# Order of the second-layer groups, GELU passes and first-batch steps in a fused attention and MLP kernel

The kernel runs on one core of a Trainium2 chip. The metric is the device time of one execution in microseconds (us): the median of several runs. Profiles and traces are of one run each (for the kernel before a further one, of 464.52 us), and the span of a profile is about 2 us shorter than the time of the same run.

## The reference

Attention whose softmax has an additional 1 in the denominator, then a two-layer MLP with exact GELU on the heads put side by side:

```
q, k, v: (8, 12, 448, 64)       # batch, heads, sequence, head size, fp32
scores = q @ k^T / 8;  m = max(scores)
e = exp(scores - m);   attn = e / (sum(e) + exp(-m) + 1e-9)
x = (attn @ v), heads joined    # 3584 tokens x 768
h = x @ w_in                    # 768 x 2048
out = gelu(h) @ w_out           # 2048 x 768, fp32
```

The kernel works in fp16 with fp32 sums and replaces the row's maximum by a constant shift.

## The kernel before

The eight batches are cut into 48 steps, one for each pair of heads. In step s the engines compute the scores and exps of pair s and the value products of pair s-1; the MLP of the batch before is laid between them as filler for the matmul engine (PE). Scores go to `st` tiles, of which there are two, and everything else of PE goes to four single banks.

```python
def scores(g, half):                       # 2 st tiles, 4 matmuls, 2 exps
    for j in (2 * half, 2 * half + 1):
        st = ps_st.tile([P, 2, 512], FP32, name="st")            # ps_st has bufs=2
        for e in range(2):
            nc.tensor.matmul(st[0:PS, e, 0:S], kt[r, c, j, :], qt[r, c]...)       # L179
        nc.scalar.activation(out=et_t[g][:, j], in_=st[...], func=AF.Exp, ...)    # L183

def attend(g):                             # 8 value products, 2 sums
    ...                                                                           # L208
    nc.tensor.matmul(den[...], ones, sum_t[g][:, e, :], ...)                      # L214
    nc.scalar.activation(out=rec, in_=den[:, 0:S], func=AF.Ln, bias=oneb)         # L218
    nc.scalar.activation(out=rec, in_=rec, func=AF.Exp, scale=-1.0)               # L219
    nc.vector.tensor_tensor(out=xt_t[b][:, c, :], in0=po[:, 0:S], in1=rec, op=ALU.mult)

def step(s, items):
    n = len(items) // 2
    scores(s, 0)
    if s < NPAIR - 1:
        transpose_on_pe(0, s + 1)
    for f in items[:n]:                    # first part of the filler
        f()
    presum(s, 0)                           # DVE adds exps for the sums
    attend(s - 1)
    scores(s, 1)
    if 2 <= s < 2 + NPAIR:
        transpose_on_pe(1, s - 2)
    for f in items[n:]:                    # second part of the filler
        f()
    presum(s, 1)
```

(The conditions for the first and last step are left out.) An item is either a chunk of the first layer (`layer1`: 6 matmuls of 448 columns, L237, there are 16 chunks to a batch) or half a row tile of the second layer (16 matmuls of 384 columns, L282). Exp and Ln share one table of ScalarE (ACT), and GELU needs another one. So GELU is done in one pass for each batch: load the table, apply it to the chunks that wait in a buffer, do the remaining chunks straight from PSUM, load the table back. The second-layer items of the batch become available after its pass.

```python
def gelu_window(b, n):
    load_table(SET_GELU)
    for f in take(len(l2)):                # second-layer items that are left
        f()
    ...                                    # n buffered chunks, then 16 - n direct ones
    load_table(SET_LN_EXP)
    l2.extend(layer2_items(b))
...
    if r < 3:
        step(s, mlp1(b, f0, f1))           # first-layer chunks as filler
    else:
        step(s, take((len(l2) - 2) // (6 - r)))   # second-layer items as filler
    if r in (1, 2) and b + 2 < B:
        transpose_on_dma(b + 2, r - 1)     # queries at r=1, keys at r=2
        if r == 2 and b + 4 < B:
            load_qk(b + 4)
    if r == 2:
        gelu_window(b, f1)                 # NBURST = 12: 12 buffered, 4 direct
```

The queries and keys of batches 0 and 1 are transposed by PE, those of later batches by the DMA queues (`transpose_on_dma`, issued by SyncE). Loads into the raw buffers are issued by GpSimd (POOL) and wait until the transposes of the batch two before have read their buffer.

The softmax here doesn't subtract the row's maximum and nothing guards it: scores larger than these inputs give would overflow.

Of the kernel before, what the change touches and what calls it, by code (L numbers as in the profile page):

```python
# [19 lines left out]
def kernel(  # L20
# [17 lines left out]
    NPAIR = H // 2  # L38
    MCH = DM // P
    FCH = DFF // P  # L40
# [28 lines left out]
    def load_table(set_id):  # L69
        nc.scalar.add_instruction(  # L70
            mybir.InstLoadActFuncSet(
                name=nc.get_next_instruction_name(),
                act_func_set_id=set_id,
                engine=mybir.EngineType.Activation,
                ins=[],
                outs=[],
            )
        )
# [7 lines left out]
    def load_heads(pool, name, tiles, key, src, h0=0, h1=H):  # L86

        if key not in tiles:
            tiles[key] = pool.tile([PS, H, NJ, D], FP16, name=name)
        nc.gpsimd.dma_start(  # L90
            out=tiles[key][:, h0:h1],
            in_=src[key[0]].rearrange("h (p j) d -> p h j d", j=NJ)[:, h0:h1],
        )

    def load_qk(b, *heads):
        for w, src in (("q", q), ("k", k)):
            load_heads(raw_pool, f"raw{w}", raw_t, (b, w), src, *heads)

    def load_v(b, *heads):
        load_heads(v_pool, "vn", v_t, (b,), v, *heads)  # L100
# [43 lines left out]
    def transpose_on_pe(b, c):  # L144
        for w in range(2):
            src = raw_t[b, "qk"[w]]
            tp = ps_bank.tile([P, NJ, PS], FP16, name="bank")
            for j in range(NJ):
                for e in range(2):
                    nc.tensor.transpose(  # L150
                        tp[e * D:(e + 1) * D, j, :], src[:, 2 * c + e, j, :], ident
                    )
            nc.vector.tensor_copy(out=qt_t[b][w][:, c], in_=tp)
# [16 lines left out]
    def scores(g, half):  # L170
        b, c = divmod(g, NPAIR)
        qt, kt = qt_t[b]
        if half == 0:
            et_t[g] = et_pool.tile([PS, NJ, 2, S], FP16, name="et")
        for j in (2 * half, 2 * half + 1):
            st = ps_st.tile([P, 2, 512], FP32, name="st")
            for e in range(2):
                r = slice(e * D, (e + 1) * D)
                nc.tensor.matmul(  # L179
                    st[0:PS, e, 0:S], kt[r, c, j, :],  # L180
                    qt[r, c].rearrange("p j s -> p (j s)"), start=True, stop=True,
                )
            nc.scalar.activation(  # L183
                out=et_t[g][:, j], in_=st[0:PS, :, 0:S], func=AF.Exp,
                bias=expb[0:PS], scale=scale,
            )

    def presum(g, part):

        et = et_t[g]  # L190
        if part == 0:
            sum_t[g] = [sum_pool.tile([PS, 2, 2, S], FP16, name="t2"), None]
        t2 = sum_t[g][0]
        nc.vector.tensor_tensor(  # L194
            out=t2[:, part], in0=et[:, 2 * part], in1=et[:, 2 * part + 1], op=ALU.add)
        if part == 1:
            sum_t[g] = sum_pool.tile([PS, 2, S], FP16, name="ksum")
            nc.vector.tensor_tensor(out=sum_t[g], in0=t2[:, 0], in1=t2[:, 1], op=ALU.add)  # L198

    def attend(g):  # L200
        b, c = divmod(g, NPAIR)
        if c == 0:
            xt_t[b] = xt_pool.tile([P, MCH, S], FP16, name="xt")
        et = et_t.pop(g)
        po = ps_bank.tile([P, 512], FP32, name="bank")
        for j in range(NJ):
            for e in range(2):
                nc.tensor.matmul(  # L208
                    po[e * D:(e + 1) * D, 0:S], v_t[b,][:, 2 * c + e, j, :], et[:, j, e, :],
                    start=(j == 0), stop=(j == NJ - 1),  # L210
                )
        den = ps_bank.tile([P, 512], FP32, name="bank")
        for e in range(2):
            nc.tensor.matmul(  # L214
                den[e * D:(e + 1) * D, 0:S], ones, sum_t[g][:, e, :], start=True, stop=True,
            )
        rec = rec_pool.tile([P, S], FP32, name="rec")
        nc.scalar.activation(out=rec, in_=den[:, 0:S], func=AF.Ln, bias=oneb, scale=1.0)  # L218
        nc.scalar.activation(out=rec, in_=rec, func=AF.Exp, scale=-1.0)  # L219
        nc.vector.tensor_tensor(out=xt_t[b][:, c, :], in0=po[:, 0:S], in1=rec, op=ALU.mult)  # L220
# [1 line left out]

    gt_even = gt_pool.tile([P, FCH, NFULL], FP16, name="gt_even")
    gt_odd = gt_pool.tile([P, FCH, LEFT + S], FP16, name="gt_odd")
    NBURST = 12
    h_t = {}

    def gelu_out(b, f0, f1):

        if b % 2 == 0:  # L230
            return [(0, NFULL, gt_even[:, f0:f1, :]), (NFULL, S, gt_odd[:, f0:f1, 0:LEFT])]
        return [(0, S, gt_odd[:, f0:f1, LEFT:])]

    def layer1(b, fc, direct=False):
        ph = ps_bank.tile([P, 512], FP32, name="bank")
        for m in range(MCH):
            nc.tensor.matmul(  # L237
                ph[:, 0:S], w_in_sb[:, m, fc * P:(fc + 1) * P], xt_t[b][:, m, :],
                start=(m == 0), stop=(m == MCH - 1),
            )  # L240
        if direct:
            for c0, c1, dst in gelu_out(b, fc, fc + 1):
                nc.scalar.activation(out=dst[:, 0, :], in_=ph[:, c0:c1], func=AF.Gelu)  # L243
        else:
            if fc == 0:
                h_t[b] = h_pool.tile([P, NBURST, S], FP32, name="hbuf")
            nc.vector.tensor_copy(out=h_t[b][:, fc, :], in_=ph[:, 0:S])  # L247

    def gelu_burst(b, f0, f1):
        for c0, c1, dst in gelu_out(b, f0, f1):  # L250
            nc.scalar.activation(out=dst, in_=h_t[b][:, f0:f1, c0:c1], func=AF.Gelu)  # L251
# [46 lines left out]
    NSTEP = B * NPAIR  # L298
    l2 = []

    def step(s, items):
        n = len(items) // 2
        if s < NSTEP:
            scores(s, 0)
        if s < NPAIR - 1:
            transpose_on_pe(0, s + 1)
        for f in items[:n]:
            f()
        if s < NSTEP:
            presum(s, 0)  # L310
        if s >= 1:
            attend(s - 1)
        if s < NSTEP:
            scores(s, 1)
        if 2 <= s < 2 + NPAIR:
            transpose_on_pe(1, s - 2)
        for f in items[n:]:
            f()
        if s < NSTEP:
            presum(s, 1)  # L320

    def mlp1(b, f0, f1):
        return [lambda fc=fc: layer1(b, fc) for fc in range(f0, f1)]

    def take(n):
        got = l2[:n]
        del l2[:n]
        return got

    def gelu_window(b, n):  # L330

        load_table(SET_GELU)
        for f in take(len(l2)):
            f()
        if b == 0:
            for i in range(FCH - n):
                gelu_burst(b, i * n // (FCH - n), (i + 1) * n // (FCH - n))
                layer1(b, n + i, direct=True)
        else:
            for f0 in range(0, n, 6):  # L340
                gelu_burst(b, f0, min(f0 + 6, n))
            for fc in range(n, FCH):
                layer1(b, fc, direct=True)
        load_table(SET_LN_EXP)
        l2.extend(layer2_items(b))
# [2 lines left out]
    transpose_on_pe(0, 0)  # L348
    alloc_qt(1)
    for s in range(NPAIR):  # L350
        step(s, [])
    for b in (2, 3):
        load_qk(b)

    for s in range(NPAIR, NSTEP + 1):
        b, r = divmod(s - 1 - NPAIR, NPAIR)
        if b < 0:
            step(s, [])
            for f in mlp1(0, 0, 2):
                f()  # L360
            continue
        f0, f1 = 4 * r, min(4 * r + 4, NBURST)
        if b == 0:
            f0, f1 = min(f0 + 2, 10), min(f1 + 2, 10)
        if r < 3:
            step(s, mlp1(b, f0, f1))
        else:
            n = len(l2) - 2
            step(s, take(n // (6 - r)))
        if r == 0 and b + 2 < B:  # L370
            load_v(b + 2)
        if r in (1, 2) and b + 2 < B:
            transpose_on_dma(b + 2, r - 1)
            if r == 2 and b + 4 < B:
                load_qk(b + 4)
        if r == 2:
            gelu_window(b, f1)

    load_table(SET_GELU)
# [36 lines left out]
```

## Time and profile before

| | before |
|---|---|
| time, three runs | 464.41 us (462.44 to 465.28) |
| span of the profile | 462.8 us |
| PE busy, idle | 431.7 us, 31.1 us |
| mean granted PE clock | 0.988 |

The prediction shows the page's busy shares, its slices and four stretches, and the timeline of PE at two GELU passes. Two lines of the list of waits of the kernel before complete them (waiting engine, tile and line; what it waited for; us in total, times, longest us):

```profile
PE st L179 <- ACT et L183: 15.7, 18, 4.8
...
ACT rec L218 <- PE bank L214: 68.2, 39, 3.9
```

The first is what PE lost to full score tiles: half of its idle time. The second is ACT's wait for the sums. It is longer, but ACT is busy only 68% of the span, so that wait costs something only where PE in its turn waits for the exps behind it.

### The profile page before, as it was taken

The page shows a single profiled execution, that of the slowest core. Times are in us where ns is not written, and L with a number is a line of the kernel's source. Part 1 is how long each engine was busy: PE and PEld are TensorE (multiplying, and loading weights), DVE is VectorE, ACT ScalarE, POOL GpSimd, SP SyncE. Part 2 cuts the span into 40 slices and gives each one's busy share as a digit, 9 for nine tenths or more (in the row PEclk, how much of TensorE's full clock was granted, in tenths as well). Part 3 has the DMA queues.
Part 4 walks back from the last instruction along what each step waited for, and adds up shares of the span by engine and source line. Part 5 has one row for each costly group of instructions (what it writes and reads, how often), then busy time and mean ns, then how long its engine had stood idle before and what let it go on. Part 6 is the DMA issues. An engine that isn't in the chain of part 4 may idle for free.

```text
span 462.8 us, 6665 instructions
## 1 busy us (share of the span) xinstructions
PE 431.7 (93%) x2720; PEld 214.2 (46%) x2720; DVE 211.2 (46%) x381; ACT 314.4 (68%) x398; POOL 32.5 (7%) x43
## 2 busy tenths in 40 slices
PE   3888996899999999799999999799999999799995
PEld 1343443354555445354555445354555445355563
DVE  1464672346714574356724574246814573330021
ACT  3778679676877669876876668776877668844200
POOL 8310020000100000000100000000000000000000
PEclk9999999799999999999999999899999999999999
DMA  8999999942792609941891606033351201020022
GB/s 103 194 206 206 209 198 186 141 69 60 109 164 55 110 3 176 96 82 47 109 164 48 115 14 142 1 61 69 59 95 43 61 2 32 4 66 3 27 77 68
DMA packets 75119, 42.51 MB, mean 92 GB/s; under 512 B 34128, under 2 KB 71504, under 8 KB 75088
## 3 DMA queue, kind: packets, MB, share of 16 engines
q0 software_dynamic: 37968, 22.81, 37.1%
q1 hardware_dynamic: 37120, 19.27, 19.8%
q8 instruction: 21, 0.34, 0.3%
q14 instruction: 10, 0.08, 0.1%
HBM read 45.61 MB, written 11.01 MB: 122 GB/s over the span
## 4 chain that ended last, share of the span: by engine, by line
PE 84%; ACT 7%; DMA 4%; DVE 2%; POOL 2%; issue 1%; POOLq 0%
PE bank L282 33%; PE bank L237 31%; PE st L179 9%; PE bank L208 8%; DMA rawk<-in_k_dram 4%; ACT et L183 3%; PE bank L214 2%; ACT L70 1%; PE bank L150 1%; ACT gt_even L243 1%; DVE ksum L198 1%; ACT gt_even L251 1%; POOL rawq L90 1%; DVE osb L286 1%; DVE t L194 1%
## 5 line engine op out<-in xcount | busy, mean ns | idle before, releaser
L183 ACT ACTIVATE et<-st,expb 112x896 f16<-112x896 f32 x192 | 181.5, 999 | 26.6 <-PE st L179 26.5
L237 PE MATMUL bank<-xt,w_in_sb 128*128 128x448 f16 x768 | 154.1, 353 | 0.6 <-ACT gt_odd L243 0.4
L237 PEld LDWEIGHTS <-w_in_sb 128*128 128x128 f16 x768 | 71.6, 98 | 75.0 <-issue 12.9
L282 PE MATMUL bank<-w_out_sb,gt_odd 128*128 128x384 f16 x512 | 87.0, 327 | 0.0
L286 DVE COPY osb<-bank 128x384 f32<-128x384 f32 x56 | 31.2, 557 | 118.9 <-PE bank L282 118.9
L179 PE MATMUL st<-tq,tk 64*112 64x448 f16 x384 | 66.2, 407 | 16.2 <-ACT et L183 15.7
L194 DVE TENSOR_TENSOR t<-et 112x896 f16<-112x896 f16 x96 | 59.3, 618 | 43.5 <-ACT et L183 43.4
L218 ACT ACTIVATE rec<-bank,oneb 128x448 f32<-128x448 f32 x48 | 30.4, 633 | 68.2 <-PE bank L214 68.2
L282 PE MATMUL bank<-w_out_sb,gt_even 128*128 128x384 f16 x384 | 69.9, 341 | 0.0
L282 PEld LDWEIGHTS <-gt_odd 128*128 128x128 f16 x512 | 48.6, 98 | 37.1 <-issue 6.1
L247 DVE COPY hbuf<-bank 128x448 f32<-128x448 f32 x82 | 50.4, 621 | 17.6 <-PE bank L237 17.1
L220 DVE TENSOR_TENSOR xt<-bank,rec 128x448 f16<-128x448 f32 x48 | 30.0, 625 | 55.7 <-ACT rec L219 55.7
L282 PEld LDWEIGHTS <-gt_even 128*128 128x128 f16 x384 | 37.6, 101 | 29.9 <-issue 8.3
L208 PE MATMUL bank<-et,vn 112*64 112x448 f16 x384 | 50.0, 387 | 0.0
L179 PEld LDWEIGHTS <-tk 64*112 64x112 f16 x384 | 22.5, 133 | 55.6 <-issue 52.1
L243 ACT ACTIVATE gt_odd<-bank 128x448 f16<-128x448 f32 (+1 forms) x46 | 19.4, 421 | 18.4 <-PE bank L237 18.1
L198 DVE TENSOR_TENSOR ksum<-t 112x896 f16<-112x896 f16 x48 | 30.0, 625 | 1.8
L208 PEld LDWEIGHTS <-vn 112*64 112x64 f16 x384 | 19.1, 117 | 23.9 <-issue 16.2
L219 ACT ACTIVATE rec<-rec 128x448 f32<-128x448 f32 x48 | 27.7, 577 | 1.5
L70 ACT ACT_TABLE_LOAD x16 | 20.5, 1283 | 1.0 <-PEq L400 0.7
L214 PE MATMUL bank<-ksum,ones 112*64 112x448 f16 x96 | 18.6, 382 | 2.0 <-DVE ksum L198 2.0
L251 ACT ACTIVATE gt_odd<-hbuf 128x2688 f16<-128x2688 f32 (+3 forms) x18 | 19.3, 1086 | 0.0
(25 smaller groups left out, 110.1 us busy)
## 6 DMA issues: line engine op xcount, KB each, us to landing
rawq<-in_q_dram POOLq DMA_DIRECT2D x7, 672.0 KB, 12.9
rawk<-in_k_dram POOLq DMA_DIRECT2D x7, 672.0 KB, 15.2
vn<-in_v_dram POOLq DMA_DIRECT2D x7, 672.0 KB, 7.6
w_in_sb<-in_moe_w_in_dram POOLq DMA_DIRECT2D x4, 768.0 KB, 22.6
w_out_sb<-in_moe_w_out_dram POOLq DMA_DIRECT2D x4, 768.0 KB, 29.8
out_dram<-osb SPq DMA_DIRECT2D x8, 336.0 KB, 2.8
out_dram<-osb SPq DMA_DIRECT2D x8, 288.0 KB, 4.3
out_dram<-osb SPq DMA_DIRECT2D x8, 240.0 KB, 3.3
```

Of the source, the lines that this page charges most:

```text
L179: nc.tensor.matmul(st[0:PS, e, 0:S], kt[r, c, j, :], qt[r, c].rearrange("p j s -> p (j s)"), start=True, stop=True,)
L183: nc.scalar.activation(out=et_t[g][:, j], in_=st[0:PS, :, 0:S], func=AF.Exp, bias=expb[0:PS], scale=scale,)
L194: nc.vector.tensor_tensor(out=t2[:, part], in0=et[:, 2 * part], in1=et[:, 2 * part + 1], op=ALU.add)
L198: nc.vector.tensor_tensor(out=sum_t[g], in0=t2[:, 0], in1=t2[:, 1], op=ALU.add)
L208: nc.tensor.matmul(po[e * D:(e + 1) * D, 0:S], v_t[b,][:, 2 * c + e, j, :], et[:, j, e, :], start=(j == 0), stop=(j == NJ - 1),)
L214: nc.tensor.matmul(den[e * D:(e + 1) * D, 0:S], ones, sum_t[g][:, e, :], start=True, stop=True,)
L218: nc.scalar.activation(out=rec, in_=den[:, 0:S], func=AF.Ln, bias=oneb, scale=1.0)
L220: nc.vector.tensor_tensor(out=xt_t[b][:, c, :], in0=po[:, 0:S], in1=rec, op=ALU.mult)
L237: nc.tensor.matmul(ph[:, 0:S], w_in_sb[:, m, fc * P:(fc + 1) * P], xt_t[b][:, m, :], start=(m == 0), stop=(m == MCH - 1),)
L247: nc.vector.tensor_copy(out=h_t[b][:, fc, :], in_=ph[:, 0:S])
L282: nc.tensor.matmul(po[:, 0:NHW], gt[:, fc, g0:g0 + P], w_out_sb[:, fc, n0:n0 + NHW], start=(fc == 0), stop=(fc == FCH - 1),)
L286: nc.vector.tensor_copy(out=osb[:, n0:n0 + NHW], in_=po[:, 0:NHW])
```

## The change

The intent is to feed PE better around the GELU passes and in the first batch. The pass comes two steps into a batch instead of three, with 8 buffered and 8 direct chunks (batch 0: one step, 6 buffered and 10 direct). With that more second-layer items are ready earlier. In the first batch a step of its own does all scores of a pair ahead of the value products of the pair before. The filler's first part is now the rounded-up half, which matters where a step has an odd number of items: a single item now comes before the value products instead of after the second scores.

```diff
-    NBURST = 12
+    NBURST = 8
+    def start_step(s):
+        scores(s, 0)
+        presum(s, 0)
+        scores(s, 1)
+        if s + 1 < NPAIR:
+            transpose_on_pe(0, s + 1)
+        if s >= 1:
+            attend(s - 1)
+        if s >= 3:
+            transpose_on_pe(1, s - 3)
+        presum(s, 1)
     def step(s, items):
-        n = len(items) // 2
+        n = (len(items) + 1) // 2
 ...
-        if 2 <= s < 2 + NPAIR:
-            transpose_on_pe(1, s - 2)
+        if s - 3 < NPAIR:
+            transpose_on_pe(1, s - 3)
 ...                                  # gelu_window: bursts of 1 (batch 0) or 4 chunks
     for s in range(NPAIR):
-        step(s, [])
+        start_step(s)
 ...
         if b == 0:
-            f0, f1 = min(f0 + 2, 10), min(f1 + 2, 10)
-        if r < 3:
+            f0, f1, last = 2, 6, 0
+        else:
+            f0, f1, last = 4 * r, 4 * r + 4, 1
+        if r <= last:
             step(s, mlp1(b, f0, f1))
         else:
-            n = len(l2) - 2
-            step(s, take(n // (6 - r)))
+            step(s, take((len(l2) - 1) // (6 - r)))
 ...
-        if r == 2:
+        if r == last:
             gelu_window(b, f1)
```

More of the change, by code (lines that the diff above doesn't have):

```diff
@@ L299 @@
     l2 = []
+    def start_step(s):
[9 more added lines that the diff above has]
+        presum(s, 1)
     def step(s, items):
-        n = len(items) // 2
+        n = (len(items) + 1) // 2
         if s < NSTEP:
             scores(s, 0)
-        if s < NPAIR - 1:
-            transpose_on_pe(0, s + 1)
         for f in items[:n]:
@@ L310, in step @@
             presum(s, 0)
-        if s >= 1:
-            attend(s - 1)
+        attend(s - 1)
         if s < NSTEP:
             scores(s, 1)
-        if 2 <= s < 2 + NPAIR:
-            transpose_on_pe(1, s - 2)
+        if s - 3 < NPAIR:
+            transpose_on_pe(1, s - 3)
         for f in items[n:]:
@@ L336, in gelu_window @@
             for i in range(FCH - n):
-                gelu_burst(b, i * n // (FCH - n), (i + 1) * n // (FCH - n))
+                if i < n:
+                    gelu_burst(b, i, i + 1)
                 layer1(b, n + i, direct=True)
         else:
-            for f0 in range(0, n, 6):
-                gelu_burst(b, f0, min(f0 + 6, n))
+            for f0 in range(0, n, 4):
+                gelu_burst(b, f0, f0 + 4)
             for fc in range(n, FCH):
@@ L350 @@
     for s in range(NPAIR):
-        step(s, [])
+        start_step(s)
     for b in (2, 3):
         load_qk(b)
-    for s in range(NPAIR, NSTEP + 1):
+    step(NPAIR, [])
+    for f in mlp1(0, 0, 2):
+        f()
+    for s in range(NPAIR + 1, NSTEP + 1):
         b, r = divmod(s - 1 - NPAIR, NPAIR)
-        if b < 0:
-            step(s, [])
-            for f in mlp1(0, 0, 2):
-                f()
-            continue
-        f0, f1 = 4 * r, min(4 * r + 4, NBURST)
         if b == 0:
-            f0, f1 = min(f0 + 2, 10), min(f1 + 2, 10)
-        if r < 3:
+            f0, f1, last = 2, 6, 0
+        else:
+            f0, f1, last = 4 * r, 4 * r + 4, 1
+        if r <= last:
             step(s, mlp1(b, f0, f1))
         else:
-            n = len(l2) - 2
-            step(s, take(n // (6 - r)))
+            step(s, take((len(l2) - 1) // (6 - r)))
         if r == 0 and b + 2 < B:
```

## The prediction

> **What bounds the kernel now.** I read the page first, its busy shares and its slices.
>
> ```profile
> PE 431.7 (93%) x2720; PEld 214.2 (46%) x2720; DVE 211.2 (46%) x381; ACT 314.4 (68%) x398; POOL 32.5 (7%) x43
> ...
> PE   3888996899999999799999999799999999799995
> ...
> PEclk9999999799999999999999999899999999999999
> ```
>
> The matmul engine is the bound: 93% busy, full in most slices. The change adds and removes no matmul (5442 TensorE rows in both programs), so its worth is what it does to PE's idle time and clock. Next I cut the span at the holes (stretch; its length; then busy us of PE, PEld, DVE, ACT, POOL; clock).
>
> ```profile
> 0.00:48.90 48.90, 36.38 (x292) 17.40 (x292) 21.53 (x48) 32.48 (x40) 17.50 (x27) 1.00 1.21 179
> ...
> 73.00:92.10 19.10, 13.03 (x65) 5.64 (x63) 3.55 (x7) 15.49 (x32) 0.93 (x1) 0.82 1.32 161
> 92.10:185.90 93.80, 93.80 (x582) 46.26 (x580) 50.21 (x89) 69.12 (x83) 5.61 (x6) 1.00 0.58 93
> 185.90:195.20 9.30, 6.92 (x51) 3.30 (x50) 2.96 (x5) 8.49 (x11) 0.00 (x0) 1.00 0.88 113
> ```
>
> PE idles 12.5 us in the first batch (bounded by ACT's exps and the first loads), 6.1 at the first GELU pass, 2.4 after each later even GELU pass, and nothing for 93.8 us between. A timeline of PE at the first pass, then at a later one (start, duration, what; in brackets the idle time before and who ended it):
>
> ```profile
> 82.53 0.40 PE L179 MATMUL st<-tq,tk 64*112 64x448 f16 x2 [4.76 <-ACT et L183]
> 83.42 0.62 PE L179 MATMUL st<-tq,tk 64*112 64x448 f16 x2 [0.50 <-ACT et L183]
> 83.98 5.30 PE L282 MATMUL bank<-w_out_sb,gt_even 128*128 128x384 f16 x16
> ```
>
> ```profile
> 189.02 0.40 PE L179 MATMUL st<-tq,tk 64*112 64x448 f16 x2 [1.43 <-ACT et L183]
> 189.92 0.40 PE L179 MATMUL st<-tq,tk 64*112 64x448 f16 x2 [0.50 <-ACT et L183]
> 190.25 2.77 PE L282 MATMUL bank<-w_out_sb,gt_even 128*128 128x384 f16 x16
> 192.95 0.59 PE L179 MATMUL st<-tq,tk 64*112 64x448 f16 x4
> ...
> 194.86 0.38 PE L214 MATMUL bank<-ksum,ones 112*64 112x448 f16 x2 [0.45 <-DVE ksum L198]
> 195.17 0.59 PE L179 MATMUL st<-tq,tk 64*112 64x448 f16 x4
> ...
> 198.40 0.59 PE L179 MATMUL st<-tq,tk 64*112 64x448 f16 x4
> ```
>
> Scores wait for a free score tile, that is for exps that stand behind ACT's GELUs and a table load. After the longer hole, 16 second-layer matmuls took 5.30 us instead of 2.77.
>
> **What the Trainium skill says.** (1) "TensorE: Matmul & The Clock Gate", Part 1: The HAM clock gate: the array runs at half rate after about one idle window of 3.4 us and returns after one busy window. The trace agrees in kind: 5.30 us at 83.98; another x16 group at 293.80 took 4.45 us after holes of 1.43 and 0.50 us, while the same holes at 189 and 398 us were followed by 2.77. So a low stretch of about 2.7 us (187.55 to 190.25, 0.66 of it busy) tripped the clock once in three. (2) The same page, Architectural detail: ScalarE is a strict FIFO. The trace shows Ln holding up the exps behind it (below). (3) "PSUM — Partial Sum Buffer", Specifications (TRN2): 8 banks of 2 KiB per partition. The kernel holds two score tiles of two banks and four single banks, so all are taken; scores cannot run further ahead than two tiles. No run shows the capacity itself; the waits above show its effect. (4) "ScalarE: Activation LUTs", What ACT_TABLE_LOAD costs: 1283 ns, as the trace has it (1283 x16); the page's drain of 1.38 us is not seen (load at 186.67, exp at 187.97). The change keeps all 16 loads.
>
> **The change, part by part.**
>
> *First batch.* Both orders give ACT four exps, then Ln and Exp of the pair before. PE's way from the exp that frees the last score tile to Ln (scores, 16 transposes, 8 value products, 2 sums) is the same either way: 32.36 to 35.87 in the trace, 3.5 us, against 1.9 us of exps. So the cadence of 6.5 us stays. The first four exps come without the wait for the second pair's loads (second two from about 8.8 instead of 10.40), and the wait of 0.93 us for batch 1's keys at 25.06 goes; but those transposes now stand between value products and the next scores (0.89 us of them and 0.66 us of scores against 1.15 us of Ln and Exp, 0.3 to 0.4 us a pair three times), and one more set is left for later (0.5 us). I put the sum at -0.5 us.
>
> *First GELU pass.* It now follows one step, with 6 buffered and 10 direct chunks. ACT needs 0.57 us for a buffered and 0.48 for a direct chunk (72.26, 72.83, 73.31), 1.05 a pair; PE needs 1.19 us for 6 matmuls. So PE leads throughout and its hole goes: 0.44+4.76+0.50+0.25 us of idle time (the last before the sums at 91.12) and about 2.9 us of half clock (5.25-2.71 on the second-layer group, the rest on scores): -8.9 us.
>
> *Later passes.* 8 direct chunks keep PE going 9.3 us instead of 4.6, and with the second-layer item now ahead of the value products PE has 2.7 us of work while ACT loads its table. The three holes of 2.38 us (1.43+0.50+0.45) and the slow group (4.45-2.77=1.7) go: -8.9 us.
>
> *Steps with one item.* The count rounds up now, so a lone second-layer item moves from after the second scores to before the value products. And with the pass two steps into the batch, lone items are spread over more steps. Counting with the change's formula: 5 in batch 0, 1 in each of batches 1, 3, 5, 3 in each of 2, 4, 6: 17; the order of the changed program shows this as eight score matmuls in a row, with nothing between. What such a step costs is seen on a before step that has an item in its first half:
>
> ```profile
> 152.30 0.63 ACT L218 ACTIVATE rec<-bank,oneb 128x448 f32<-128x448 f32 x1 [2.06 <-PE bank L214]
> 152.97 0.58 ACT L219 ACTIVATE rec<-rec 128x448 f32<-128x448 f32 x1
> 153.45 1.89 ACT L183 ACTIVATE et<-st,expb 112x896 f16<-112x896 f32 x2
> ```
>
> Ln waits while the item delays the sums. There a second item keeps PE busy meanwhile; with a lone one nothing does. The loop from exp end to exp end: last scores 0.05+0.33 (189.87 to 190.25), item 2.70 (148.42 to 151.12), value products and sums to Ln 1.18 (to 152.30), Ln and Exp 1.15, two exps 1.89: 7.30 us. PE's own work in it is 0.52+2.70+0.78+0.29+0.52=4.81 us; the same step took 5.45 us before (192.95 to 198.40). So PE stalls 2.5 us in 15 of these steps, 2.0 in batch 0's first, which still has transposes, and 0.45 in the last, which has no scores after it: +40 us.
>
> *Clock.* Each stall is a stretch of 3.0 us with 0.66 us of scores, thinner than the one that tripped one time in three. I estimate 4 in 10 of 16, at about 2 us each (1.7 and 2.5 were seen): +13 us.
>
> Sum: 464.4-0.5-8.9-8.9+40+13 = 499 us.
>
> **Rivals.** (a) *The holes close and nothing opens*: about 446 us. For it: both GELU holes are real, ACT is only 68% busy, and a lone-item step needs 4.93 us of ACT against 4.81 of PE. Against it: Ln is ahead of the exps in ACT's queue, and Ln needs the sums behind the item; two score tiles allow no more lead. (b) *The stalls come but the clock holds*: 486 us. For it: two of three such holes kept the clock. Against it: these are longer. (c) *The clock trips nearly every time*: 16 times 2 us gives 518. For it: in the first 48 us score pairs take 0.62 us instead of 0.40 throughout, although PE is 74% busy, so the array leaves the slow state unwillingly. Against it: an item of 2.7 to 5.3 us is dense. (d) *The first batch warms the array earlier*, since work is more contiguous: up to 3 us less. I give it little weight. (e) *A load becomes late*: the second-layer weights land 30 us after issue at 28.72, about 59 us, and the first item would come near 76: hidden anyway. Batch 2's transposes move behind the pass, but have four steps left.
>
> **Range and chances.** The stall arithmetic is firm to perhaps 5 us; the clock term runs from 0 to 32, mostly 5 to 25. So 485 to 514. Slower by over 2% (over 473.7) needs only half of the stalls: 0.92. Within 2%: 0.05, should something overlap that I think serial. Faster: 0.03.
>
> **What would show it.** Right: PE without idle time at the first GELU pass; its busy share down to about 87%; a new wait of scores on exps, in pairs of about 1.7 and 0.6 us, some 16 times; Ln waiting about 2.4 us for the sums in the same steps; second-layer groups of 4 to 5.3 us with clock slices under 9. Wrong: lone-item steps near 5.5 us, which would mean that the scores or the Ln do not wait as I have it; or clock slices all at 9, which would take away the last 13 us.

## The result

The changed kernel took 502.07 us (median of four runs, 498.43 to 503.11) beside 463.9 us of the kernel before in the same rounds. The ratio is 1.081 (95% interval 1.074 to 1.088). Ratios here and below are the mean time of one kernel's runs over that of the kernel before in the same rounds, so they are not quite the ratio of the medians. Executions over 1.5% slower than the fastest of the same kernel are left out of the means.

The page of the changed kernel, its busy shares and two rows of its slices:

```profile
PE 442.5 (88%) x2720; PEld 219.1 (44%) x2720; DVE 196.6 (39%) x353; ACT 318.3 (63%) x442; POOL 32.4 (6%) x43
...
PE   4787988758989999779998999869998999889996
...
PEclk9998997879999999879998999899999999989999
```

PE executes the same 2720 instructions, but its share of the span fell from 93% to 88%, and the clock row has nine slices under 9 where it had two. The list of waits says what PE waited for:

```profile
PE st L179 <- ACT et L183: 40.7, 42, 1.8
PE st L179 <- DMA tk<-re: 5.7, 1, 5.7
...
ACT rec L218 <- PE bank L214: 104.9, 48, 4.6
```

PE's wait for exps rose by 25.0 us, in many short pieces (42 instead of 18, none longer than 1.8 us), and a wait of 5.7 us for transposed keys is new. Ln's wait for the sums rose by 36.7 us. Cut into stretches (start and end; length; busy us and (x) instructions of PE, PEld, DVE, ACT, POOL; clock, DMA share, GB/s), the changed kernel reads:

```profile
0.00:47.19 47.19, 32.21 (x277) 16.64 (x277) 20.97 (x45) 31.95 (x39) 17.48 (x27) 0.96 1.21 179
47.19:68.35 21.16, 21.16 (x135) 10.41 (x132) 8.76 (x17) 16.58 (x40) 0.00 (x0) 1.00 1.01 161
68.35:116.04 47.69, 33.76 (x191) 15.28 (x191) 16.49 (x30) 26.50 (x34) 5.60 (x6) 0.82 0.84 121
319.00:375.60 56.60, 49.88 (x303) 24.29 (x300) 24.21 (x43) 39.07 (x49) 0.93 (x1) 0.97 0.31 58
```

The second line is the first GELU pass with the step before it: PE is busy for all of it, and the hole of 4.76 us is gone. The third is the five steps with one item that follow: PE idles 13.9 us of 47.7, and at a clock of 0.82. The last runs from a step with one item over the next, odd pass: idle time is in its single-item steps alone.

The timeline of PE in such steps (start, duration, what; in brackets the idle time before and what ended it), first one whose item is slow, then two whose items are not:

```profile
321.97 0.40 PE L179 MATMUL st<-tq,tk 64*112 64x448 f16 x2 [0.50 <-ACT et L183]
322.30 4.46 PE L282 MATMUL bank<-w_out_sb,gt_even 128*128 128x384 f16 x16
...
331.28 2.77 PE L282 MATMUL bank<-w_out_sb,gt_even 128*128 128x384 f16 x16
...
335.05 0.59 PE L179 MATMUL st<-tq,tk 64*112 64x448 f16 x4
337.36 0.40 PE L179 MATMUL st<-tq,tk 64*112 64x448 f16 x2 [1.72 <-ACT et L183]
338.25 0.40 PE L179 MATMUL st<-tq,tk 64*112 64x448 f16 x2 [0.50 <-ACT et L183]
338.58 2.77 PE L282 MATMUL bank<-w_out_sb,gt_even 128*128 128x384 f16 x16
```

From item to item it is 338.58 - 331.28 = 7.30 us. The four scores at 335.05 are the second half of one pair, and the first half of the next stands right behind them. These need the two score tiles back, and ACT has only just come to the exps that free them. ACT at the same time:

```profile
335.17 0.63 ACT L218 ACTIVATE rec<-bank,oneb 128x448 f32<-128x448 f32 x1 [2.47 <-PE bank L214]
...
336.31 3.69 ACT L183 ACTIVATE et<-st,expb 112x896 f16<-112x896 f32 x4
```

ACT idles 2.47 us because Ln needs the sums, which stand behind the item; then PE idles because the exps stand behind Ln. Each engine waits in turn for the other. Eleven of the second-layer groups behind such a stall, one of them behind the wait for keys below, took 3.70 to 5.16 us instead of 2.77.

The wait for keys, on PE:

```profile
105.43 1.00 PE L179 MATMUL st<-tq,tk 64*112 64x448 f16 x4 [5.74 <-DMA tk<-re]
106.36 5.16 PE L282 MATMUL bank<-w_out_sb,gt_even 128*128 128x384 f16 x16
```

The SyncE queue that issues those transposes (of batch 2: first the queries', then the keys'), in the kernel before and in the changed kernel:

```profile
68.47 7.63 SPq L162 DMA_TRANSPOSE tq<-re  x1
76.15 12.59 SPq L162 DMA_TRANSPOSE tk<-re  x1
```

```profile
78.20 7.90 SPq L162 DMA_TRANSPOSE tq<-re  x1
87.31 11.87 SPq L162 DMA_TRANSPOSE tk<-re  x1
```

The schedule now puts them behind the first pass, and they start 10 and 11 us later. They are slow to issue in both kernels: batch 3's queries at 132.31 us, with one load beside them (issued at 132.51), take 3.09 us. The keys land 18.1 us after their issue, where it was 16.0 before. So most of the lateness against the kernel before is the later start. GpSimd's loads of batch 3's queries, before and after:

```profile
56.90 0.94 POOL L90 DMA_DIRECT2D rawq<-in_q_dram  x1 [19.37 <-PE bank L150]
```

```profile
74.28 0.94 POOL L90 DMA_DIRECT2D rawq<-in_q_dram  x1 [36.47 <-PE bank L150]
```

This load overwrites batch 1's raw queries and so waits for the last transposes by PE (L150). The change puts these behind the first GELU pass, the load starts 17.4 us later, and it runs beside batch 2's transposes. In the kernel before loads ran beside them too: batch 3's values, issued at 58.76 us, landed 20.1 us later, and batch 4's queries were issued at 68.67.

The span grew by 38.5 us (462.8 to 501.3), of which 27.7 is idle time of PE and 10.8 busy time. The parts, read from the two timelines:

| part | PE idle, us | PE busy, us |
|---|---|---|
| first batch, up to the first layer | +2.5 | -4.2 |
| first GELU pass: hole gone | -6.5 | |
| later even passes: holes gone | -7.1 | |
| 16 stalls in steps with one item, and 0.4 in the last such step | +35.4 | |
| the longer wait for keys in one of them (5.74 instead of 2.22) | +3.5 | |
| 11 slow second-layer groups (sum of durations over 2.77) | | +17.2 |
| slow groups of before at its passes, with scores | | -4.6 |
| all else (score pairs that run apart or slowly) | | +2.4 |
| sum (rounding apart) | +27.8 | +10.8 |

### The profile page after: what moved, and what is told of

Its sections match the earlier page's. It is cut to its first block, busy times and chain, and to the rows that moved or that the text cites. A ratio compares the mean times of both kernels' runs of the same rounds, so it can differ in the third digit from the quotient of the medians.

```text
span 501.3 us, 6697 instructions
## 1 busy us (share of the span) xinstructions
PE 442.5 (88%) x2720; PEld 219.1 (44%) x2720; DVE 196.6 (39%) x353; ACT 318.3 (63%) x442; POOL 32.4 (6%) x43
## 4 chain that ended last, share of the span: by engine, by line
PE 81%; ACT 11%; DMA 4%; issue 2%; DVE 1%; ACTq 0%; DVEq 0%; POOLq 0%
PE bank L282 32%; PE bank L237 30%; PE bank L208 8%; ACT et L183 8%; PE st L179 8%; DMA tk<-re 4%; ACT rec L218 2%; PE bank L214 2%; PE bank L150 1%; DMA rawq<-in_q_dram 1%; ACT rec L219 0%; DVE ksum L198 0%; DVE t L194 0%; DVE tk L153 0%; DVE tq L153 0%
## 5 line engine op out<-in xcount | busy, mean ns | idle before, releaser
L237 PE MATMUL bank<-xt,w_in_sb 128*128 128x448 f16 x768 | 151.2, 353 | 0.0
L179 PE MATMUL st<-tq,tk 64*112 64x448 f16 x384 | 67.4, 403 | 47.4 <-ACT et L183 40.7
L237 PEld LDWEIGHTS <-w_in_sb 128*128 128x128 f16 x768 | 72.9, 98 | 72.6 <-issue 7.7
L282 PE MATMUL bank<-w_out_sb,gt_odd 128*128 128x384 f16 x512 | 90.4, 334 | 0.0
L282 PE MATMUL bank<-w_out_sb,gt_even 128*128 128x384 f16 x384 | 80.7, 374 | 0.0
L282 PEld LDWEIGHTS <-gt_even 128*128 128x128 f16 x384 | 40.5, 110 | 37.2 <-issue 18.6
L243 ACT ACTIVATE gt_odd<-bank 128x448 f16<-128x448 f32 (+1 forms) x74 | 28.9, 395 | 22.8 <-PE bank L237 22.8
L247 DVE COPY hbuf<-bank 128x448 f32<-128x448 f32 x54 | 33.4, 622 | 13.1 <-PE bank L237 12.7
L219 ACT ACTIVATE rec<-rec 128x448 f32<-128x448 f32 x48 | 27.7, 576 | 1.5
L243 ACT ACTIVATE gt_even<-bank 128x384 f16<-128x384 f32 x34 | 16.7, 490 | 10.3 <-PE bank L237 10.1
```

The source lines that it names most:

```text
L237: nc.tensor.matmul(ph[:, 0:S], w_in_sb[:, m, fc * P:(fc + 1) * P], xt_t[b][:, m, :], start=(m == 0), stop=(m == MCH - 1),)
L243: nc.scalar.activation(out=dst[:, 0, :], in_=ph[:, c0:c1], func=AF.Gelu)
L247: nc.vector.tensor_copy(out=h_t[b][:, fc, :], in_=ph[:, 0:S])
L282: nc.tensor.matmul(po[:, 0:NHW], gt[:, fc, g0:g0 + P], w_out_sb[:, fc, n0:n0 + NHW], start=(fc == 0), stop=(fc == FCH - 1),)
```

## The experiments

All gave correct results. "Before" and "after" name the two kernels; each run is compared with runs of before on the same chip (463.4 to 464.3 us as median).

**e1: after, rounded down.** A lone item goes back behind the second scores.

```diff
-        n = (len(items) + 1) // 2
+        n = len(items) // 2
```

> The changed kernel, but a lone second-layer item goes back behind the second scores (count rounded down). My theory: the 7.30 us loop of a lone-item step becomes the 5.45 us loop of the kernel before, so the 16 stalls of 2.5 us and their clock trips go; in return the hole of about 2.4 us after each of the 7 GELU passes is back, since every pass is now followed by a lone item. Sum: 445 (all holes closed) + 9 other lone steps x 0.64 + 7 x 2.4 + two or three trips x 1.7 = about 472, range 466 to 478. Rival (the spreading of the items over more steps is at fault, not their place in the step): 490 or more.

Measured: 478.99 us, ratio 1.035 (1.031 to 1.039), 23 us less than after. The single-item steps take 5.44 us, and their items 2.77, save for one of 3.12 us behind the wait shown below and one of 4.45 at 250.86 us, behind the holes of 1.37 and 0.50 us after a pass. So the place of the item costs most of the loss. But the time misses its range by a microsecond, and not for a reason that I had written down:

```profile
106.64 0.99 PE L179 MATMUL st<-tq,tk 64*112 64x448 f16 x4 [12.58 <-DMA tk<-re]
```

PE comes to batch 2's keys at 94.06 us (106.64 - 12.58), in after at 99.69 (105.43 - 5.74), but the keys are no earlier than in after (their transposes start at 80.55 and 89.94 us). What the steps save ahead of this point is given back here.

**e2: before, rounded up.** The one line alone, the other way round.

```diff
-        n = len(items) // 2
+        n = (len(items) + 1) // 2
```

> The kernel before with the count of the first half rounded up, and nothing else. Theory: its 8 lone-item steps get the 7.30 us loop in place of 5.45 us, but those right behind a GELU pass fill the hole there (2.4 us) in exchange; worked out by batch: +2.6 us in batches 2 and 4, +0.6 in 6, about -2 in batch 0, and some 6 stalls of which 6 in 10 trip the clock for 1.7 us, against one such trip before: 468 to 474. Rival (the place of the item does no harm by itself, only the longer row of lone items does): 464.

Measured: 466.9 us, ratio 1.011 (1.004 to 1.018): slower, though just under the range. Its single-item steps show the same 7.30 us. Only two groups were slow in the profiled run, so the clock term was smaller than I allowed; and a wait of 2.32 us for batch 2's keys, which the kernel before doesn't have, appears at 92.55 us. The same line costs much more in after than in before; after's schedule has 17 steps with a single item and before's 8, four of them right behind a pass, where the item also fills a hole. That this is the whole reason isn't shown.

**e3: before, with the new first batch alone.** `start_step`, and batch 1's PE transposes one step later.

```diff
     for s in range(NPAIR):
-        step(s, [])
+        start_step(s)
-        if 2 <= s < 2 + NPAIR:
-            transpose_on_pe(1, s - 2)
+        if s - 3 < NPAIR:
+            transpose_on_pe(1, s - 3)
```

> The kernel before with the first batch's new order alone. My prediction had put this part at -0.5 us; the trace of the changed kernel shows the first layer starting 1.7 us earlier (47.19 against 48.92) with 0.5 us of transposes left for later, so about -1.2 us: 463 (ratio 0.996 to 0.999). Rival (the new order overlaps exps and value products better in every pair): -3 us or more.

Measured in five rounds: 465.11 us, ratio 1.0031 (1.0002 to 1.0059), that is +1.4 us. The first layer starts at 48.47 us instead of 48.92; the transposes left over take 0.5 us back, and a wait of 1.34 us for batch 2's keys appears at 95.40 us. So this part brings nothing by itself. It makes the keys later by little: their transposes start at 69.07 and 76.90 us, less than 1 us behind the kernel before, though batch 3's load comes 7.5 us later (64.36). The rival of -3 us falls, and so does the size that I read out of after's trace.

**e4: after, with work in the stalls.** Seven matmuls whose result nobody reads follow the second scores of single-item steps, so that PE is neither idle nor in need of anything.

```diff
+        if s < NSTEP and len(items) == 1:
+            junk = ps_bank.tile([P, 512], FP32, name="bank")
+            for i in range(7):
+                nc.tensor.matmul(junk[:, 0:S], w_in_sb[:, 0, 0:P], w_in_sb[:, 1, 0:S],
+                                 start=True, stop=True)
```

> The changed kernel with 7 matmuls of 448 columns that nobody reads (about 1.35 us) in each lone-item step after the second scores, inside the stall of 2.2 us. Theory (the stall is set by Ln and the exps, and the slow item groups are the clock tripped by the thin stretch): the stall stays as long, item groups return to 2.77 us, the granted clock to 0.98 or more, the time drops by the 17.8 us that the slow groups of the trace add up to, less what the wait for the transposed keys still trips: 482 to 488. Rival (matmul time is the limit in these steps, or the slow groups have another cause): the time does not drop, or rises by up to 16 x 1.35 = 22 us.

The timeline of PE in one step:

```profile
82.17 1.50 PE L328 MATMUL bank<-w_in_sb 128*128 128x448 f16 x7
83.95 0.40 PE L179 MATMUL st<-tq,tk 64*112 64x448 f16 x2 [0.29 <-ACT et L183]
84.85 0.40 PE L179 MATMUL st<-tq,tk 64*112 64x448 f16 x2 [0.50 <-ACT et L183]
85.18 2.77 PE L282 MATMUL bank<-w_out_sb,gt_even 128*128 128x384 f16 x16
```

Measured: 493.21 us, ratio 1.063 (1.060 to 1.067), about 9 us less than after, with 119 matmuls more. The junk takes the place of idle time, steps stay at 7.30 us (item starts at 77.88, 85.18 and 92.48), and every item of a single-item step but one takes 2.77 us; the exception follows the wait for keys. So the slow groups come from the idle time in the stall and not from the item itself, and the clock is a separate cost. The time misses the expected range: the wait for keys grew from 5.74 to 10.23 us, with a group of 5.14 us behind it. Saving time ahead of that wait only lengthens the wait.

**e5: after, with batch 1's last PE transposes one step sooner**, ahead of the first GELU pass.

```diff
-        if s - 3 < NPAIR:
+        if s - 3 < NPAIR - 1:
             transpose_on_pe(1, s - 3)
+        if s - 4 == NPAIR - 3:
+            transpose_on_pe(1, NPAIR - 1)
```

> The changed kernel with the last PE transposes of batch 1 one step earlier, ahead of the first GELU pass, so that the load of batch 3's q and k is released there instead of at 74 us. Theory: the wait of 5.74 us for the transposed keys of batch 2 at 105 us came of these loads running beside the DMA transposes; it goes, and the scores there wait about 2.2 us as elsewhere: -3.5 us, and up to 2.8 us more if the clock holds there: 495 to 499, and no wait on tk. Rival (the transposes are late because they are issued late, after the pass): the wait stays, 502.

Measured: 494.76 us, ratio 1.066 (1.062 to 1.070). The load of batch 3's queries starts at 54.27 us instead of 74.28. Batch 2's transposes start about when they did in after (78.26 and 85.50 us; in after 78.20 and 87.31) but take 3.68 and 6.31 us to issue instead of 7.90 and 11.87, the keys land 14.2 us after their issue instead of 18.1, and the wait for them falls to 2.87 us; it was expected to go. So loads beside the transposes slow them, and half of the wait in after comes from that. e11 below takes out the other cause, the late start, and leaves loads beside them. One of the four runs, of 501.45 us, is slow and isn't in the ratio; the median of the other three is 493.53, 1.5 us under the range. The gain of 8.5 us is more than the 2.9 us of that wait; in the profiled run 7 groups (one of the first layer) were slow instead of 11, which would give the rest, but the number of slow groups differs from run to run.

**e6: after, with the second scores ahead of the value products** in single-item steps, e5's transposes, and batch 2's DMA transposes ahead of the first pass. The item stays where the change put it.

```diff
+        ahead = len(items) == 1 and s < NSTEP
+        if ahead:
+            scores(s, 1)
         attend(s - 1)
-        if s < NSTEP:
+        if s < NSTEP and not ahead:
             scores(s, 1)
 ...
+        if b == 0 and r == 0:
+            transpose_on_dma(2, 0)
+            transpose_on_dma(2, 1)
```

> The changed kernel with those early transposes, and in lone-item steps the second scores moved ahead of the value products, so that their exps stand ahead of Ln in ACT's queue; the lone item stays where the change put it, in the first half. Theory (Ln, waiting for the sums behind the item, holds up the exps in the queue): the loop from exp to exp becomes 0.38 + 2.70 + 0.44 + 1.89 = 5.4 us instead of 7.30, PE waits under 1 us a step, the clock holds: 445 with all holes closed + 16 x 0.6 = 455 (451 to 459), faster than the kernel before. Rival (two score tiles are too few whatever the order): 480 or more.

Measured: 460.36 us, ratio 0.994 (0.991 to 0.997): 1.4 us above the range. The steps take 5.43 us, as expected. But a wait of 3.75 us for keys has moved to batch 4 (at 197.94 us), with a group of 4.98 us behind it.

**e7: e1 with e6's earlier transposes**, that is the item back behind the second scores, and the keys in time.

```diff
-        n = (len(items) + 1) // 2
+        n = len(items) // 2
 ...                                    # transposes of batches 1 and 2 as in e6
```

> The first run (count rounded down) again, with batch 1's last PE transposes before the first GELU pass and batch 2's two DMA transposes issued before that pass as well. The first run took 479 because its scores of batch 2 waited 12.58 us for transposed keys that landed at 106 us. Theory: that wait goes and all else stays: 466 (464 to 470), no wait on tk over 1 us. Rival (the transposes land at about 100 us whatever the issue order, since the loads of weights and batches fill the queues): 472 or more.

Measured: 467.62 us, ratio 1.010 (1.006 to 1.014), in the expected range. Rounding down and earlier transposes together give back 34 of the 38 us. But it is still slower than before: with a lone item behind the second scores the holes of 1.43 and 0.50 us after the passes are back, now after odd passes too (1.37 and 0.50), and one wait of 1.68 us for keys is left, where none over 1 us was expected.

**e8: e6 with the item cut in two**: 13 of its matmuls before the value products, 3 after them.

```diff
         for f in items[:n]:
-            f()
+            f(0, SPLIT) if ahead else f()          # SPLIT = 13
 ...
         attend(s - 1)
+        if ahead:
+            items[0](SPLIT, FCH)
```

> As the run with the second scores ahead, with the lone item cut: 13 of its 16 matmuls before the second scores, 3 after the sums. Theory: the second scores are ready before ACT has done the first exps, so that ACT never waits and the loop falls to its own work, 1.15 + 4 exps at 0.945 = 4.93 us, against 5.4: 16 x 0.45 = 7 us less than that run, about 448 (445 to 452). Rival (the cut costs as much as it saves, or other waits take over): no difference between the two.

Measured: 460.58 us, ratio 0.993 (0.990 to 0.997), the same as e6 and a miss. Two waits for keys, 4.42 us at 93 us and 3.70 at 200 us, took what the cut may have given. Nothing follows on the cut itself.

**e11 and e10: the loads in order, without and with the second scores ahead.** Both start from after with e5's transposes. In the program, both DMA transposes of batch 2 come ahead of the first pass, those of later batches one step sooner, and the loads of raw queries and keys behind them.

```diff
-    for b in (2, 3):
-        load_qk(b)
+    load_qk(2)
 ...
-        if r in (1, 2) and b + 2 < B:
-            transpose_on_dma(b + 2, r - 1)
-            if r == 2 and b + 4 < B:
-                load_qk(b + 4)
+        if b == 0 and r == 0:
+            transpose_on_dma(2, 0)
+            transpose_on_dma(2, 1)
+        if b > 0 and r in (0, 1) and b + 2 < B:
+            transpose_on_dma(b + 2, r)
+        if b == 0 and r == 3:
+            load_qk(3)
+        if r == (2 if b else 4) and b + 4 < B:
+            load_qk(b + 4)
```

e10 has e6's lines for `ahead` in addition.

> The changed kernel with its loads put in order and its steps left as the change has them: batch 1's last PE transposes and batch 2's DMA transposes before the first GELU pass, the DMA transposes of later batches one step earlier, the loads of q and k of batches 3 and 4 two to three steps later. Theory: no wait on transposed keys, all else as in the changed kernel: 446 + 16 stalls of 2.49 + ten trips of 1.6 = 502 - 6 = about 496 (492 to 499).

> As that, with the second scores ahead of the value products in lone-item steps: one move apart from the run above. Theory: 16 x (7.30-5.43) = 30 us and the trips, 16 us, go: 450 (447 to 454), no step loop over 5.5 us. The earlier run with this move took 460, of which 3.8 us of waiting for transposed keys of batch 4 and 2.2 us of half clock behind it should go now. Rival: something else is behind the 460, and it stays there.

Measured: e11 493.08 us, ratio 1.061 (1.056 to 1.066), and no wait for keys in its list. GpSimd runs ahead of the steps and still starts its loads as soon as their buffers are free (batch 3's at 54.49 us), and batch 2's transposes still take 7.19 and 12.81 us to issue; but they start at 63.69 and 70.93 us, some 15 us sooner than in after, and that is enough. e10 454.47 us, ratio 0.979 (0.975 to 0.983): half a microsecond above its range, with one wait of 0.93 us for keys left and 5.58 us for the first such step behind a pass. The two programs differ by one thing, the place of four score matmuls and their two exps in the single-item steps, and their times by 38.6 us. The timeline of PE in one such step of e10:

```profile
80.60 2.77 PE L282 MATMUL bank<-w_out_sb,gt_even 128*128 128x384 f16 x16
83.30 0.59 PE L179 MATMUL st<-tq,tk 64*112 64x448 f16 x4
83.82 0.95 PE L208 MATMUL bank<-et,vn 112*64 112x448 f16 x8
...
85.70 0.40 PE L179 MATMUL st<-tq,tk 64*112 64x448 f16 x2 [0.42 <-ACT et L183]
86.03 2.77 PE L282 MATMUL bank<-w_out_sb,gt_even 128*128 128x384 f16 x16
```

ACT in the same step:

```profile
85.54 0.63 ACT L218 ACTIVATE rec<-bank,oneb 128x448 f32<-128x448 f32 x1
```

ACT now has the exps of the second scores in its queue ahead of Ln (from 83.74 us), and works on them while PE does the value products. Ln follows them without idle time, where ACT idled 2.47 us before it in after. From item to item it is 5.43 us, PE waits 0.42 us, and no item is slow. The two orders of the same work differ by 7.30 - 5.43 = 1.87 us a step, and by what the clock loses.

**e9: e10 with the item cut in 13 and 3**, as in e8.

> As that, with the lone item cut 13 to 3. Theory: the loop of 4.94 to 5.1 us that the earlier run with the cut showed in batch 0 stands in all 16 lone-item steps, and its two waits for transposed keys (4.42 and 3.70 us, with 1.1 and 2.6 us of half clock behind them) go: 460.6 - 11.8 = 449, some 0.4 x 16 = 6 us less than the run without the cut if that one has no waits either, so 444 to 450. Rival (the earlier pair, 460.36 and 460.58, was level because the cut gains nothing): level again.

Measured: 454.68 us, ratio 0.979 (0.975 to 0.982), level with e10 and a miss. The later single-item steps fell to 4.94 and 5.10 us, but the first one behind a pass rose from 5.58 to 5.97, and one wait for keys of 3.43 us returned.

**e12: e9 with the cut only in steps not right behind a pass.**

```diff
-            step(s, take((len(l2) - 1) // (6 - r)))
+            step(s, take((len(l2) - 1) // (6 - r)), cut=r > last + 1)
```

> The run with the cut item, but the item is cut only in lone-item steps that do not stand right behind a GELU pass. Why the cut was level (454.68 against 454.47): in the traces its step loop is 0.33 to 0.49 us shorter in later lone steps, but the first step behind each of the seven passes is 0.39 us longer, because there the second scores wait for the table load anyway and the 3 last matmuls come on top; and one wait for transposed keys was 3.43 instead of 0.93 us. Theory: without those seven losses 9 x 0.4 = 3.6 us are left: 451 (449 to 453.5), ratio 0.967 to 0.977. Rival (the cut gives nothing that lasts): 454.5, ratio 0.979.

Measured in five rounds: 452.92 us, ratio 0.977 (0.974 to 0.981), at the edge of the range, with one wait of 1.4 us for keys. Its interval overlaps those of e10 and e9, so whether the cut is worth anything stays open. What is settled is that e10 beats both kernels: its ratio and those of e9 and e12 lie 1.7% to 2.6% below 1 by their intervals.

## Why the prediction was right

The predicted 499 us stands beside 502.07, inside the range, and the main sign and size came by the mechanism that the prediction named. Three of its readings don't stand as written, though its sum doesn't rest on them. The 5442 rows of TensorE are in no page: both show 2720 matmuls and 2720 weight loads. The stall holds two score pairs of 0.40 us, so 0.8 us of scores and not 0.66. And the slow array of the first 48 us is that of one run: in e2, with the same first batch, a group of transposes took 0.36 us at 19.7 us, with slow stretches after it. By its steps:

- *First batch, -0.5 us: the wrong way by a little.* In the profile of after it is -1.2 us (first layer 1.7 us sooner, less 0.5 of transposes), but that is the array's clock, which rose sooner in that run: PE is busy for 4.2 us less and idle for 2.5 more. When it rises differs between the runs: with the old first batch the first layer begins at 48.92 us in before and at 45.28 in e2, with the new one between 44.36 (e9) and 48.47 (e3). So one trace can't give a term of 1 us here, and whether the new order makes an early rise likelier (rival (d)) stays open. Alone in e3 this part was +1.4 us, with an interval from 0.1 to 2.7 us.
- *First GELU pass, -8.9 us: right.* PE is busy for 21.16 of 21.16 us there.
- *Later passes, -8.9 us: right.* The holes of 7.1 us and the slow group of 1.7 us are gone.
- *Steps with one item, +40 us: right.* The loop is the predicted 7.30 us to the second digit. PE's idle time in it is 2.22 us and not 2.5; the rest of the stall shows as busy time, because scores that come in two pairs take 0.40 and 0.40 us where four together take 0.59. That it is the item's place is shown by e1 and e7, and by e10 against e11, which leaves the item and moves the scores.
- *Clock, +13 us: right in kind, sized too low.* The term that was off is "4 in 10 of 16, at about 2 us each". The profiled run had 11 slow groups with 17.2 us, 1.6 us each. One of them (5.16 us) is behind the wait for keys. e4 shows that the idle time trips the clock: with 1.5 us of work in the stall, no item of those steps was slow except behind that wait.
- *Rival (e), a load becomes late, "hidden anyway": wrong.* I looked at the weights, and took four steps to be enough for batch 2's transposes. They start 10 and 11 us later than before. The keys then need 18.1 us to land, with batch 3's loads beside them, which the change delays by 17 us; PE comes to them 12.4 us after their issue. Moving batch 3's loads away (e5) leaves a wait of 2.87 us; starting the transposes 15 us sooner, with loads still beside them (e11), leaves none. Together the two causes cost 3.5 us of waiting and a slow group behind it (5.16 - 2.77 = 2.4 us) in the profiled run; removing the wait entirely in e11 gave 9 us, in which the changed count of slow groups (5 instead of 11) has its part. How the 9 us divide between the two is not settled.

The late keys and the larger clock term are 3.5 + 4.2 = 7.7 us that the sum lacked. The spans differ by 38.5 us where the steps of the prediction add up to 34.7, so half of this was made good by the other terms, each of which came out a little lower.

## What to carry to other kernels

When two engines hand tiles back and forth, look for an instruction in a strict queue (here Ln) that needs late work of the other engine: what stands behind it in its queue waits too, so moving four matmuls and two exps ahead of it was worth 38.6 us of 493 here. Filler belongs where the waiting engine has something to do meanwhile, and should be counted for odd and lone items. Take a slow wait out and look again: the transposed keys cost between 0 and 12.6 us here depending on when they were issued, what ran beside them and how soon the steps came.

## What the Trainium skill lacked or had wrong

- "TensorE: Matmul & The Clock Gate", Part 1: The HAM clock gate. It has the array return to full rate after about 3.4 us of sustained work, in windows that run free of the kernel. In the kernel before PE issued without a gap from 33.00 to 37.67 us, and its groups of transposes took 0.59 us at both ends (0.36 to 0.39 us later) and stayed slow until about 48 us. A stretch of 4.67 us need not hold a whole window, so this doesn't contradict the page; whether the 32 transposes among its 46 matmuls count as the products do was not tested. The granted clock in the profile's slices reads 9 there, so only the durations show it. The page has the array slow down after an idle window of about 3.4 us; here stalls of 3.0 us that contained 0.8 us of scores were followed by a slow group 10 times of 15 in one run (the one with the wait for keys left out), and 1.5 us of matmuls inside prevented it. It doesn't say how thin work may be before it counts as idle.
- "DMA: Bandwidth & Descriptors", DMA Transpose (X-bar). It gives no time for issuing a transpose beside other transfers. The same transpose of a batch's queries or keys kept SyncE's queue for 3.1 us with one load beside it and, in before and after, for 7.6 to 12.6 us with several loads running, where the data landed 16 to 18 us after the issue.
- "ScalarE: Activation LUTs", What ACT_TABLE_LOAD costs. The drain of 1.38 us on top of the load was not seen in the changed kernel either: the exps end at 186.63 us, the load starts at 186.65, and GELU starts at 187.94.
